# A fused attention and feed-forward kernel: the row's threshold word moves from VectorE to GpSimd

## The chip, the cores and the metric

One core of one Trainium2 chip runs the whole program. The metric is device time in microseconds of one execution. The profile names the engines PE (TensorE, its weight loads as PEld), DVE (VectorE), ACT (ScalarE), POOL (GpSimd) and SP (SyncE, which here only issues transfers).

## What is computed

Attention in which a row keeps only the scores within `tau` of its maximum, over 8 batches of 8 heads, 576 positions, 64 dimensions, and behind it a dense layer pair of 512 to 2048 to 512 with the activation h * tanh(softplus(h)), in float32:

```
scores = scale * q @ k^T                       # per head 576 x 576
thresh = max(scores, axis=-1) - tau
scores = where(scores >= thresh, scores, -1e9)
attn   = exp(scores - max(scores)); attn = attn / (sum(attn) + 1e-9)
x      = (attn @ v), heads side by side        # 4608 tokens x 512
h      = x @ w_in                              # 512 -> 2048
out    = (h * tanh(log1p(exp(h)))) @ w_out     # 2048 -> 512
```

## The kernel before

Attention works on pairs of heads. A pair is cut into 9 tiles of 128 query rows, 32 pairs give 288 tiles (`NT`), and the loop over `g` in `attention_moe` issues one tile's stages per turn, each stage some turns behind the one before. Between them it hands out the first matrix product of earlier batches (`gemm1`, through `advance`), so that TensorE has work while a tile passes through the other engines. After the last tile come the rest of `gemm1` and the second product, which have no attention work beside them.

Every engine runs its instructions in the order in which the loop issues them: `Engines` wraps TensorE, VectorE, ScalarE and GpSimd, and `InOrder` ties each instruction to the one before it on its engine. Its `method(...)` call is line 95, so nearly every row of the profile reads L95 and is told apart by its tiles.

What tile `g` goes through, by the names in the profile:

- `scores` writes the 128 x 576 scores to one of two PSUM buffers `s`. TensorE can start tile g+2 only when tile g's buffer has been read by the masking.
- `row_max` (VectorE, `st<-s`, TENSOR_REDUCE) puts the negated row maximum into word 0 of `st`, a small tile of 8 words a row, of which three exist in turn.
- `exponential` makes two words from it: the exponential's bias (word 2, `st<-st`) and the threshold (word 1, `st<-st,back`, where `back` holds tau in unscaled units). Then ScalarE writes `e<-s,st`.
- `masked` (VectorE, `p<-s,st,e`, SCALAR_TENSOR_TENSOR) compares the scores with the threshold, multiplies by `e` and sums the row. From tile 54 (`UNV`) on GpSimd then makes a 128x1 word `un` of the sum (`st<-st` on POOL), before that VectorE makes it in `total`.
- `normalise` (VectorE RECIPROCAL, then GpSimd `p<-p,st`, 128x576) scales the tile; it is issued one turn later, so in turn g it scales tile g-1.
- `transposes`, two turns behind, turns `p` into `tp` and `t`; ScalarE and VectorE split these into `hi`, `lo` and `tk` three turns behind; `values` multiplies by v into `y`, and the results are gathered by `x<-x,yo` on GpSimd.

GpSimd also makes the low parts of the loaded q, k and v (`q<-r,q`, `k<-r,k`, `vs<-r,vs`), of x (`xl<-x,xh`) and, up to about 200 us, of the first weights (`w1l<-dec,w1h`, `dec<-dec`).

In one turn of the loop the calls that matter stand in this order, after `begin(g + 1)` for early tiles: row_max(g), total(g-1), exponential(g), normalise(g-1), the split parts of tile g-3, the gathers and low parts, masked(g), and then `gemm1` with `begin(g + 1)` in its middle.

Of the kernel before, what the change touches and what calls it, by code (L numbers as in the profile page):

```python
# [9 lines left out]
ALU = mybir.AluOpType  # L10
# [175 lines left out]
def attention_moe(tc, q, k, v, tau, w_in, w_out, out):  # L186
    nc = tc.nc
    from contextlib import ExitStack

    with ExitStack() as outer:  # L190
# [8 lines left out]
        back = cst.tile([P, 1], F32, name="back")  # L199

        nc = Engines(tc)
        with ExitStack() as first:
# [21 lines left out]
            with ExitStack() as att:  # L224
# [22 lines left out]
                def rows(x, step):  # L247

                    flat = x.rearrange("p a b -> p (a b)")
                    return flat[:, :2 * step].rearrange("p (a b) -> p a b", a=2)[:, :, :HL]  # L250
# [162 lines left out]
                def exponential(s, st, e):  # L413
                    nm = st[:, 0:1]
                    nc.vector.tensor_scalar(st[:, 2:3], nm, SCALE, None, ALU.mult)
                    nc.vector.tensor_scalar(st[:, 1:2], nm, -1.0, back, ALU.mult, ALU.subtract)
                    nc.scalar.activation(rows(e, HL), rows(s, 512 - 2 * G), AF.Exp, bias=st[:, 2:3], scale=SCALE)

                def masked(g, s, st, e, p):
# [224 lines left out]
                for g in range(NT + 5):  # L644
# [32 lines left out]
                    if g < NT:  # L677
                        exponential(tiles[g]["s"], tiles[g]["st"], tiles[g]["e"])
# [384 lines left out]
```

## Time and profile before

| | |
|---|---|
| Runs | 1316.25, 1318.91, 1318.0 us, median 1318.0 us |
| Profiled execution | 1316.2 us, of it 1314.4 us span |
| TensorE clock granted | 0.998 of full speed |
| Busy share of the span | PE 98%, PEld 94%, DVE 87%, ACT 78%, POOL 57% |
| Threshold word on VectorE | 288 instructions, 204 ns each |
| 128x1 word `un` on GpSimd | 234 instructions, 220 ns each |
| Scaling on GpSimd | 288 instructions, 836 ns each |

The span runs from the first to the last instruction. Attention fills it to about 900 us; the rest is the second product. A row in order of time gives start and duration in microseconds, the engine, the operation, what it writes from what it reads, a count, and in brackets the idle time ahead of it with what ended that. A group gives its busy time and the mean in ns, then the idle time ahead of all its members and what ended most of it. A wait gives the sum, how often, and the longest.

### The profile page before, as it was taken

Reading aid. Unit: us, or ns where it says so; the run is one execution under the profiler, and the core shown is the slowest. Engines: PE = TensorE matmul, PEld = TensorE weight load, DVE = VectorE, ACT = ScalarE, POOL = GpSimd, SP = SyncE. Lnnn points to the kernel's source line nnn. Section 1 sums busy time; section 2 is a strip of 40 time slices with the busy share of each in tenths; the row PEclk is TensorE's granted clock in tenths of the full one; section 3 lists DMA queues with packets and bytes.
Section 4 is the critical chain, followed back from the end, with each engine's and each line's share of the span. In section 5 each row is a group of like instructions: output and inputs, shape, how many; then the busy total and the mean of one; then the engine's idle time right before and its main releaser. Section 6 shows DMA issues by size and latency. Waiting matters only on the chain.

```text
span 1314.4 us, 30410 instructions
## 1 busy us (share of the span) xinstructions
PE 1282.1 (98%) x9875; PEld 1241.6 (94%) x9875; DVE 1140.2 (87%) x2943; ACT 1029.1 (78%) x2320; POOL 746.0 (57%) x1080
## 2 busy tenths in 40 slices
PE   8998899999999999999999999999999999999998
PEld 7766899999999999999999999999999999999998
DVE  7999999999999999999999999997978666778764
ACT  6889888888888888888888888877767667567562
POOL 4779888888788887888888888774100000000000
PEclk9999999999999999999999999999999999999999
DMA  5334455444444444444445444425645454553440
GB/s 187 114 104 139 150 152 147 129 126 143 127 148 134 139 130 131 148 138 132 136 125 155 129 138 143 118 91 168 226 141 158 124 139 135 161 153 111 115 121 33
DMA packets 171917, 178.68 MB, mean 136 GB/s; under 512 B 46576, under 2 KB 139760, under 8 KB 171504
## 3 DMA queue, kind: packets, MB, share of 16 engines
q1 hardware_dynamic: 171760, 176.74, 45.4%
q8 instruction: 79, 1.29, 0.4%
q14 instruction: 78, 0.64, 0.2%
HBM read 109.05 MB, written 49.28 MB: 120 GB/s over the span
## 4 chain that ended last, share of the span: by engine, by line
PE 70%; DVE 17%; ACT 9%; issue 4%; POOL 0%; DMA 0%; SPq 0%; DVEq 0%; ACTq 0%; POOLq 0%
PE h L95 20%; PE y L95 15%; PE x L95 11%; PE s L95 8%; PE z L95 7%; DVE st L95 6%; PE tp L95 6%; DVE p L95 4%; ACT e L95 3%; DVE dec L95 2%; DVE lo L95 2%; PE hx L95 1%; ACT hi L95 1%; DVE tk L95 1%; ACT dec L95 1%
## 5 line engine op out<-in xcount | busy, mean ns | idle before, releaser
L95 PE MATMUL h<-xh,w1h 128*128 128x288 f32 x976 | 295.0, 302 | 2.5 <-ACT yo L95 1.1
L95 PE MATMUL h<-xh,w1l 128*128 128x288 f32 x976 | 292.4, 300 | 0.0
L95 PE MATMUL h<-xl,w1h 128*128 128x288 f32 x976 | 288.3, 295 | 0.3 <-DVE xl L95 0.3
L95 POOL TENSOR_SCALAR p<-p,st 128x576 f32<-128x576 f32 x288 | 240.9, 836 | 65.0 <-DVE st L95 42.1
L95 ACT ACTIVATE e<-s,st 128x580 f32<-128x580 f32 x288 | 215.0, 747 | 62.3 <-DVE st L95 56.6
L95 DVE SCALAR_TENSOR_TENSOR p<-s,st,e 128x580 f32<-128x580 f32 x288 | 236.2, 820 | 18.9 <-ACT e L95 7.3
L95 DVE TENSOR_REDUCE st<-s 128x1 f32<-128x580 f32 x288 | 217.8, 756 | 0.9
L95 PE MATMUL s<-k,q 128*128 128x290 f32 (+1 forms) x1056 | 196.2, 309 | 9.5 <-DVE p L95 8.8
L95 DVE TENSOR_TENSOR ring<-un,ring 128x512 fp32r<-128x512 f32 x252 | 156.8, 683 | 53.6 <-ACT ring L95 53.6
L95 DVE TENSOR_TENSOR lo<-tp,hi 128x512 fp32r<-128x512 f32 (+1 forms) x280 | 173.1, 627 | 25.1 <-ACT hi L95 22.9
L95 PEld LDWEIGHTS h<-xh,w1h 128*128 128x128 f32 x976 | 184.0, 188 | 6.4 <-ACT yo L95 4.2
L95 PEld LDWEIGHTS h<-xl,w1h 128*128 128x128 f32 x976 | 183.8, 188 | 0.5 <-DVE xl L95 0.5
L95 PEld LDWEIGHTS h<-xh,w1l 128*128 128x128 f32 x976 | 183.7, 188 | 0.0
L95 PE MATMUL tp<-ident,p 128*128 128x128 f32 x1152 | 173.8, 273 | 10.1 <-DVE lo L95 5.6
L95 PEld LDWEIGHTS s<-k,q 128*128 128x128 f32 x1056 | 157.6, 189 | 22.8 <-DVE p L95 19.7
L95 ACT CAST hi<-tp 128x512 fp32r<-128x512 f32 (+1 forms) x280 | 150.0, 546 | 35.5 <-PE tp L95 31.6
L95 ACT CAST ring<-un 128x512 fp32r<-128x512 f32 x252 | 138.3, 618 | 33.7 <-DVE un L95 32.8
L95 PEld LDWEIGHTS tp<-ident,p 128*128 128x128 f32 x1152 | 137.7, 140 | 21.8 <-POOL k L95 6.9
L95 PE MATMUL x<-ring,un 128*128 128x256 f32 x1296 | 154.6, 278 | 0.6 <-ACT ring L95 0.6
L95 PEld LDWEIGHTS x<-ring,un 128*128 128x128 f32 x1296 | 152.1, 188 | 0.8 <-ACT ring L95 0.8
L95 PE MATMUL y<-hi,vs 128*128 128x256 f32 (+1 forms) x448 | 132.0, 317 | 3.0 <-ACT hst L95 2.4
L95 PE MATMUL y<-lo,vs 128*128 128x256 f32 (+1 forms) x448 | 121.8, 295 | 0.0
(88 smaller groups left out, 2570.9 us busy)
## 6 DMA issues: line engine op xcount, KB each, us to landing
hd<-hst SPq DMA_DIRECT2D x128, 288.0 KB, 2.6
r<-q SPq DMA_DIRECT2D x120, 160.0 KB, 2.6
r<-k SPq DMA_DIRECT2D x120, 160.0 KB, 2.2
out_t<-ost SPq DMA_DIRECT2D x36, 256.0 KB, 2.2
r<-v SPq DMA_DIRECT2D x56, 160.0 KB, 2.3
dec<-w_in SPq DMA_DIRECT2D x32, 256.0 KB, 2.8
un<-hd SPq DMA_DIRECT2D x16, 512.0 KB, 5.4
kph<-k SPq DMA_DIRECT2D x56, 144.0 KB, 3.0
```

The source lines that it names most:

```text
L95: made = method(*args, **kwargs)
```

## The change

The threshold word is issued on GpSimd instead of VectorE, at the same place in the code. The operation and its operands stay.

```
@@ exponential(s, st, e)
                     nm = st[:, 0:1]
                     nc.vector.tensor_scalar(st[:, 2:3], nm, SCALE, None, ALU.mult)
-                    nc.vector.tensor_scalar(st[:, 1:2], nm, -1.0, back, ALU.mult, ALU.subtract)
+                    nc.gpsimd.tensor_scalar(st[:, 1:2], nm, -1.0, back, ALU.mult, ALU.subtract)
                     nc.scalar.activation(rows(e, HL), rows(s, 512 - 2 * G), AF.Exp, bias=st[:, 2:3], scale=SCALE)
```

Since `exponential(g)` is called ahead of `normalise(g-1)`, the word stands on GpSimd behind the word `un` of tile g-1 and ahead of the scaling of tile g-1. The masking of tile g, which stayed on VectorE, reads it from there. The order on TensorE, ScalarE and SyncE is the same as before.

On GpSimd, in the middle of attention (the stretch about 399 to 408 us of the profile before), first before:

```order
L95 TENSOR_TENSOR x<-x,yo 64x320
L95 TENSOR_TENSOR q_6198<-r,q_6198 64x320 x2
L95 TENSOR_SCALAR st<-st 128x1
L95 TENSOR_SCALAR p<-p,st 128x576
L95 TENSOR_SCALAR st<-st 128x1
L95 TENSOR_SCALAR p<-p,st 128x576
L95 TENSOR_TENSOR x<-x,yo 64x320
L95 TENSOR_TENSOR q_6201<-r,q_6201 64x320
L95 TENSOR_SCALAR st<-st 128x1
L95 TENSOR_SCALAR p<-p,st 128x576
```

and now, on the same engine and at the same place:

```order
L95 TENSOR_TENSOR x<-x,yo 64x320
L95 TENSOR_TENSOR q_6198<-r,q_6198 64x320 x2
L95 TENSOR_SCALAR st<-st 128x1
L95 TENSOR_SCALAR st<-st,back 128x1
L95 TENSOR_SCALAR p<-p,st 128x576
L95 TENSOR_SCALAR st<-st 128x1
L95 TENSOR_SCALAR st<-st,back 128x1
L95 TENSOR_SCALAR p<-p,st 128x576
L95 TENSOR_TENSOR x<-x,yo 64x320
L95 TENSOR_TENSOR q_6201<-r,q_6201 64x320
L95 TENSOR_SCALAR st<-st 128x1
L95 TENSOR_SCALAR st<-st,back 128x1
```

A 128x1 instruction has come between the word `un` and the scaling in each tile; the splits and gathers ahead of them in the queue are those of before.

On VectorE over the same tiles, before (`lo`, `tk` are the split parts of an older tile):

```order
L95 TENSOR_REDUCE st<-s_141 128x1
L95 TENSOR_SCALAR st<-st 128x1
L95 TENSOR_SCALAR st<-st,back 128x1
L95 RECIPROCAL st<-st 128x1
L95 TENSOR_TENSOR lo<-tp,hi 128x4x128
L95 SCALAR_TENSOR_TENSOR p,st<-s_141,st,e_142 128x580
L95 TENSOR_REDUCE st<-s_135 128x1
L95 TENSOR_SCALAR st<-st 128x1
L95 TENSOR_SCALAR st<-st,back 128x1
```

and now, on VectorE over these tiles:

```order
L95 TENSOR_REDUCE st<-s_141 128x1
L95 TENSOR_SCALAR st<-st 128x1
L95 RECIPROCAL st<-st 128x1
L95 TENSOR_TENSOR lo<-tp,hi 128x4x128
L95 SCALAR_TENSOR_TENSOR p,st<-s_141,st,e_142 128x580
L95 TENSOR_REDUCE st<-s_135 128x1
L95 TENSOR_SCALAR st<-st 128x1
L95 RECIPROCAL st<-st 128x1
```

The reciprocal, on which the scaling on GpSimd waits, now stands one instruction earlier; the masking (`p,st<-...`) waits for a word from another engine.

More of the change, by code (lines that the diff above doesn't have):

```diff
@@ L415, in exponential @@
                     nc.vector.tensor_scalar(st[:, 2:3], nm, SCALE, None, ALU.mult)
-                    nc.vector.tensor_scalar(st[:, 1:2], nm, -1.0, back, ALU.mult, ALU.subtract)
+                    nc.gpsimd.tensor_scalar(st[:, 1:2], nm, -1.0, back, ALU.mult, ALU.subtract)
                     nc.scalar.activation(rows(e, HL), rows(s, 512 - 2 * G), AF.Exp, bias=st[:, 2:3], scale=SCALE)
```

## The prediction

> **What bounds the kernel now.** I read the page's head first, then the table of busy time by stretch, then the waits of the long attention stretch, then the order of time on VectorE, GpSimd and TensorE over three tiles.
>
> ```profile
> span 1314.4 us, 30410 instructions
> PE 1282.1 (98%) x9875; PEld 1241.6 (94%) x9875; DVE 1140.2 (87%) x2943; ACT 1029.1 (78%) x2320; POOL 746.0 (57%) x1080
> ...
> core 0: us, PE busy (x) PEld busy (x) DVE busy (x) ACT busy (x) POOL busy (x), PEclk, DMA share, GB/s
> 0.00:100.00 100.00, 91.62 (x504) 72.15 (x504) 86.14 (x306) 77.39 (x193) 66.37 (x87) 1.00 0.44 135
> 100.00:200.00 100.00, 88.58 (x598) 79.81 (x598) 95.19 (x297) 85.37 (x221) 89.00 (x114) 0.98 0.50 146
> 200.00:870.00 670.00, 663.72 (x5095) 652.66 (x5094) 627.08 (x1837) 579.46 (x1408) 562.38 (x839) 1.00 0.46 136
> 870.00:1314.00 444.00, 438.23 (x3684) 436.98 (x3682) 331.76 (x507) 286.83 (x501) 28.24 (x42) 1.00 0.46 134
> ```
>
> The mean of 57% for GpSimd hides two stages. From 870 us on it does almost nothing, and of the 288 tiles only 9 are left there (288 less the 61 and 218 counted below), which I leave out. From 200 to 870 us TensorE is 99% busy and sets the pace, VectorE is at 94% and GpSimd at 84%. From 100 to 200 us TensorE is at 89%, VectorE at 95%, GpSimd at 89%: there the two helpers set the pace. So the question is how much room GpSimd really has.
>
> ```profile
> L95 POOL TENSOR_SCALAR p<-p,st 128x576 f32<-128x576 f32 x218 | 180.4, 828 | 38.3 <-DVE st L95 19.9 <-DMA kph<-k 1.7 <-PE y L95 0.4
> L95 POOL TENSOR_SCALAR st<-st 128x1 f32<-128x1 f32 x218 | 48.0, 220 | 19.9 <-DVE p L95 0.5
> ...
> POOL x L95 <- ACT yo L95: 35.2, 46, 1.2
> ACT e L95 <- DVE st L95: 29.1, 53, 1.4
> POOL p L95 <- DVE st L95: 19.9, 37, 0.9
> PEld s L95 <- DVE p L95: 0.4, 1, 0.4
> ```
>
> These are GpSimd's groups and the waits from 200 to 870 us: 218 tiles, so 3.07 us a tile. Of the 107.6 us in which GpSimd isn't busy (670 - 562.4), 19.9 us stand ahead of the 128x1 instruction with almost no releaser: 0.09 us of issue each. The waits with a name come to 35.2 + 19.9 + 1.7 and a few small ones, which I put at 62 us, 0.28 us a tile. That is all the room there is. TensorE waits for a masked tile once in this stretch (0.4 us).
>
> **The change part by part.** Three tiles in order of time, the three engines mixed:
>
> ```profile
> 399.88 1.72 POOL L95 TENSOR_TENSOR q<-r,q 64x320 fp32r<-64x320 f32 x2
> 401.51 0.82 DVE L95 SCALAR_TENSOR_TENSOR p<-s,st,e 128x580 f32<-128x580 f32 x1
> 401.69 0.22 POOL L95 TENSOR_SCALAR st<-st 128x1 f32<-128x1 f32 x1
> 402.00 0.82 POOL L95 TENSOR_SCALAR p<-p,st 128x576 f32<-128x576 f32 x1
> 402.26 0.76 DVE L95 TENSOR_REDUCE st<-s 128x1 f32<-128x580 f32 x1
> 402.91 0.21 POOL L95 TENSOR_SCALAR st<-st 128x1 f32<-128x1 f32 x1
> 403.05 0.15 DVE L95 TENSOR_SCALAR st<-st 128x1 f32<-128x1 f32 x1
> 403.12 0.20 DVE L95 TENSOR_SCALAR st<-st,back 128x1 f32<-128x1 f32 x1
> 403.24 0.15 DVE L95 RECIPROCAL st<-st 128x1 f32<-128x1 f32 x1
> 403.43 0.69 DVE L95 TENSOR_TENSOR lo<-tp,hi 128x512 fp32r<-128x512 f32 x1
> 403.57 0.82 POOL L95 TENSOR_SCALAR p<-p,st 128x576 f32<-128x576 f32 x1 [0.45 <-DVE st L95]
> 404.44 0.69 PE L95 MATMUL s<-k,q 128*128 128x290 f32 x4
> 404.78 0.82 DVE L95 SCALAR_TENSOR_TENSOR p<-s,st,e 128x580 f32<-128x580 f32 x1
> 405.63 0.87 POOL L95 TENSOR_TENSOR x<-x,yo 64x320 f32<-64x320 f32 x1 [1.24 <-ACT yo L95]
> 406.32 0.29 PE L95 MATMUL s<-kph,qph 128*128 128x290 f32 x1
> 406.46 0.88 POOL L95 TENSOR_TENSOR q<-r,q 64x320 fp32r<-64x320 f32 x1
> 407.34 0.82 DVE L95 SCALAR_TENSOR_TENSOR p<-s,st,e 128x580 f32<-128x580 f32 x1
> 407.43 0.21 POOL L95 TENSOR_SCALAR st<-st 128x1 f32<-128x1 f32 x1
> ```
>
> What VectorE gains: the threshold word starts at 403.12 and the reciprocal at 403.24, so its place in the queue is worth 0.12 us and not its 0.20 us. Over 288 tiles that is 35 us of VectorE's time. From 200 us on it lies beside TensorE, which is the bound, so I cost it at nothing there; its cover is TensorE's 99%.
>
> What GpSimd pays: the nearest row is its own 128x1 instruction, 0.22 us long. The scaling behind it starts 0.31 us after it does (401.69 to 402.00), so I take 0.31 us a tile: 218 x 0.31 = 67.6 us from 200 to 870 us. The lower end is its duration alone, 218 x 0.22 = 48 us; the upper end is the row of the early stage below, 0.43 us, 94 us. The threshold word has a tensor as second operand, which the nearest row has not; on VectorE that made 0.20 out of 0.15 us, so the lower end is unlikely. The Trainium skill, Perfetto Trace Analysis, section GPSIMD Engine Instruction, says that a GpSimd instruction's reported span is unreliable and should be timed by start-to-start spacing. By spans alone GpSimd would need 48 us of its 62 us of waits and the main stage would cost nothing; by spacing it needs more than it has. The rows agree with spacing.
>
> The new wait: VectorE's masking step now waits for GpSimd, and behind it in VectorE's queue stand the next row maximum, the exponential's bias and the split parts. At 401.51 us the masking ran while GpSimd was still at the two q splits (399.88 + 1.72 = 401.60). With the change the word could run only behind the 128x1 at 401.69, about where the scaling stands at 402.00, and end at 402.2: the masking starts 0.7 us late. For the next tile the word is ready about 403.5, a microsecond ahead of the masking at 404.78. For the one at 407.34 GpSimd is busy to 407.34 and its 128x1 starts at 407.43, so the word ends near 408.0, again 0.65 us late. Such delays don't reach TensorE at once: the masking that ends at 402.33 (401.51 + 0.82) frees the bank of the scores that start at 404.44, 2.1 us of slack, and the one that ends at 405.60 the scores at 406.32, 0.7 us. So a late tile is absorbed as long as GpSimd catches up. That it doesn't, on average, is what costs.
>
> How much of the 62 us GpSimd can use: the waits for yo (35.2 us in 46, 0.77 us each) come once in 4.7 tiles, in which the new instruction adds 1.46 us, so they vanish whole. The waits for the reciprocal (19.9 us in 37) hang on the same row maximum that the new word waits for, and if the masking is late that moves too; I let a third vanish, 7 us. With 4 us of the small ones, 46 us are used: 67.6 - 46 = 21.6 us longer. The bounds are 5.6 us (all 62 used) and 67.6 us (none).
>
> The early stage, up to 200 us, where most tiles have no other 128x1 on GpSimd:
>
> ```profile
> 148.68 1.72 POOL L95 TENSOR_TENSOR q<-r,q 64x320 fp32r<-64x320 f32 x2
> 150.47 0.74 POOL L95 TENSOR_TENSOR w1l<-dec,w1h 128x256 fp32r<-128x256 f32 x1
> 151.19 0.98 POOL L95 TENSOR_SCALAR p<-p,st 128x576 f32<-128x576 f32 x1
> ...
> L95 POOL TENSOR_SCALAR p<-p,st 128x576 f32<-128x576 f32 x29 | 25.1, 864 | 2.8 <-DVE st L95 2.2
> ...
> L95 POOL TENSOR_SCALAR p<-p,st 128x576 f32<-128x576 f32 x61 | 53.1, 870 | 22.3 <-DVE st L95 19.9 <-DVE dec L95 1.5
> ...
> PEld s L95 <- DVE p L95: 19.9, 30, 1.7
> PE s L95 <- DVE p L95: 9.0, 16, 1.5
> ```
>
> The first three rows are GpSimd back to back: the scaling starts 0.02 us before the step ahead of it ends. With an issue gap of 0.09 us on both sides the word would push it by about 0.42 us. From 100 to 200 us there are 29 tiles (the first count): 12 us more work against 11 us that GpSimd isn't busy. The second count and the waits below it are of the stretch from 0 to 200 us: TensorE waits 28.9 us there for masked tiles, so here time on the helpers is time of the kernel. The first 32 tiles (61 - 29) leave GpSimd room (66% busy), and half of VectorE's 32 x 0.12 us may show: -2 us. For the second hundred I let half the 12 us show: +6 us. Together +4 us, between -7 us (61 x 0.12, all gained) and +12 us.
>
> Sum: 1316.2 us (1314.4 us of span and 1.8 us around it) + 21.6 + 4 = 1341.8 us. The median of the runs shown, 1318.0 us, lies 1.8 us above the profiled execution: 1343.6, say 1344 us, 2.0% slower.
>
> **The rivals.**
> Absorbed: the word costs GpSimd no more than its waits, 0.22 us or less, and the 0.7 to 2.1 us of slack ahead of the scores take what is left. Then 1318 us, within about 3 us; it speaks for it that TensorE waited 0.4 us for masked tiles from 200 to 870 us. 0.2% is about what a measurement can tell from no change.
> Faster: VectorE's relief shows wherever TensorE waited for it. The place is the first 200 us, the price 61 x 0.12 = 7 us: 1311 us. It decides for this if GpSimd comes to the word before VectorE gets to the masking, as in the tile at 404.78; two tiles out of three above speak against.
> Lockstep: GpSimd has to wait for each row maximum and VectorE for GpSimd in each tile, so no wait is used up: +68 +10 us, 1396 us. The uneven work between two scalings speaks for it (two splits ahead of 401.69, none ahead of 402.91), the slack of 0.7 to 2.1 us against.
> Blocked port: GpSimd's word and VectorE's bias word start on the same row maximum, and one could hold the other up by 0.15 to 0.22 us. Over 61 early tiles that is at most 13 us, 1357 us with the forecast. The 128x1 at 402.91 on GpSimd ran beside the one at 403.05 on VectorE, and neither was longer than usual:
>
> ```profile
> L95 DVE TENSOR_SCALAR st<-st x217: 153/154/157, 203.5 to 867.4; 128x1 f32<-128x1 f32 x109
> ```
>
> The Trainium skill, SBUF — State Buffer, section Who interferes with whom, says that a VectorE instruction in a two-port mode and a GpSimd instruction lock each other out for the whole of it. The longest of 217 here is 157 ns, so no row bears the lock out for these shapes.
>
> **How the numbers follow.** Chances: the forecast (1327 to 1375 us, from a main stage between +5.6 and about +50) 0.64; lockstep (1375 to 1400) 0.12; blocked port on top 0.04; absorbed 0.10; faster 0.10. Absorbed splits into 0.08 within 0.2% and 0.02 slower. Slower 0.64 + 0.12 + 0.04 + 0.02 = 0.82. The range leaves out the faster case and the far part of lockstep: 1318 to 1380 us; the forecast's own is 1327 to 1375.
>
> **What would show it.** Right: from 200 us on the same work takes about 22 us longer, GpSimd is over 90% busy there, its waits for yo nearly gone, and a new wait of VectorE's p for GpSimd's st leads the list. TensorE's share in that stage falls to about 96%, with waits of s for p. The stage from 870 us on keeps its length. Wrong: if the new 128x1 group has no gap of its own around it, if VectorE's p waits little for it, or if the scalings start earlier, the sum falls to the rival it points to.

## The result and the profile after

The changed kernel takes 1379.98 us (median; 1379.79 to 1380.73) against 1317.99 us: a ratio of 1.0474, 95% interval 1.0459 to 1.0490, 62.0 us slower. The prediction had 26 us. Page head, chain and the table of busy time by stretch of the kernel after, with the stretches set so that the middle one holds about as many tiles:

```profile
span 1378.9 us, 30197 instructions
PE 1310.5 (95%) x9875; PEld 1248.2 (91%) x9875; DVE 1105.1 (80%) x2655; ACT 1023.1 (74%) x2320; POOL 833.7 (60%) x1368
...
PE 34%; DVE 32%; POOL 15%; ACT 11%; issue 6%; DMA 1%; POOLq 0%; SPq 0%; DVEq 0%; ACTq 0%
...
0.00:100.00 100.00, 90.23 (x491) 70.84 (x491) 81.33 (x263) 75.02 (x186) 72.74 (x116) 1.00 0.43 130
100.00:200.00 100.00, 87.45 (x547) 77.64 (x546) 87.13 (x254) 79.91 (x204) 89.86 (x131) 0.93 0.47 137
200.00:920.00 720.00, 681.06 (x5059) 649.83 (x5057) 593.99 (x1608) 570.24 (x1404) 626.06 (x1050) 1.00 0.42 126
```

The chain that ended last ran on TensorE for 34% of the span; before, this line read:

```profile
PE 70%; DVE 17%; ACT 9%; issue 4%; POOL 0%; DMA 0%; SPq 0%; DVEq 0%; ACTq 0%; POOLq 0%
```

From 200 us on no engine is busy all the time: TensorE fell from 99% to 95%, VectorE from 94% to 82%, and GpSimd rose only from 84% to 87%. Of GpSimd's 93.9 us that aren't busy, waits with a name make up about 44 us; the rest are short gaps without one. The engines wait for each other. Groups of GpSimd and waits from 200 to 920 us:

```profile
L95 POOL TENSOR_SCALAR p<-p,st 128x576 f32<-128x576 f32 x216 | 179.6, 832 | 1.3 <-POOL st L95 0.3
L95 POOL TENSOR_SCALAR st<-st,back 128x1 f32<-128x1 f32 x216 | 66.3, 307 | 29.5 <-DVE st L95 11.7
L95 POOL TENSOR_SCALAR st<-st 128x1 f32<-128x1 f32 x217 | 50.9, 235 | 21.3 <-DVE p L95 0.8
...
ACT e L95 <- DVE st L95: 117.3, 156, 2.3
DVE p L95 <- POOL st L95: 80.0, 91, 2.6
POOL x L95 <- ACT yo L95: 26.0, 46, 0.9
PEld s L95 <- DVE p L95: 14.7, 18, 1.5
```

216 tiles in 720 us are 3.33 us a tile; before, 218 in 670 us were 3.07. The difference, 0.26 us, times 218 is 57 us. Counted by the start of the 62nd masking (197.8 us before, 207.6 now) and of the 280th (868.5 and 933.8), the change costs 9.8 us up to the first and 55.5 us between the two; behind them nothing is added. (The two profiled spans lie 64.5 us apart, a little more than the medians.) The new wait of VectorE's masking for GpSimd leads VectorE's own waits with 80.0 us, and the exponential's wait for VectorE went from 29.1 to 117.3 us. GpSimd still waits 26.0 us for yo (35.2 before). Two turns of the loop in order of time, GpSimd, VectorE and ScalarE mixed, some rows left out:

```profile
449.18 0.87 POOL L95 TENSOR_TENSOR vs<-r,vs 128x320 fp32r<-128x320 f32 x1
450.15 0.24 POOL L95 TENSOR_SCALAR st<-st 128x1 f32<-128x1 f32 x1
450.48 0.30 POOL L95 TENSOR_SCALAR st<-st,back 128x1 f32<-128x1 f32 x1
450.76 0.83 POOL L95 TENSOR_SCALAR p<-p,st 128x576 f32<-128x576 f32 x1
450.82 0.82 DVE L95 SCALAR_TENSOR_TENSOR p<-s,st,e 128x580 f32<-128x580 f32 x1 [0.95 <-POOL st L95]
451.56 1.15 DVE L95 SCALAR_TENSOR_TENSOR dec<-dec 128x256 uint32<-128x256 uint32 x1
452.64 0.75 DVE L95 TENSOR_REDUCE st<-s 128x1 f32<-128x580 f32 x1
453.43 0.15 DVE L95 TENSOR_SCALAR st<-st 128x1 f32<-128x1 f32 x1
453.68 0.74 ACT L95 ACTIVATE e<-s,st 128x580 f32<-128x580 f32 x1 [2.24 <-DVE st L95]
454.75 0.42 ACT L95 COPY yo<-y 64x320 f32<-64x320 f32 x1
455.25 0.87 POOL L95 TENSOR_TENSOR x<-x,yo 64x320 f32<-64x320 f32 x1 [0.42 <-ACT yo L95]
```

This is a ring. GpSimd comes late to the threshold word (450.48), so VectorE stands idle for 0.95 us ahead of the masking; behind the masking in VectorE's queue stand the next row maximum and bias word (453.43), so ScalarE stands idle for 2.24 us ahead of the exponential; behind that in ScalarE's queue stands the copy yo (454.75); and for yo GpSimd, late itself, waits another 0.42 us. In this turn a step of the second weights (`dec`, 1.15 us) also stands between the masking and the row maximum; only 16 of the 216 tiles have one. Without it the links are the same: at 511.59 us a masking started after 0.96 us of idle time, the exponential at 513.38 after 1.86 us, and the gather at 514.96 after 0.22 us of waiting for yo.

### The profile page after: what moved, and what is told of

Read it like the earlier page. It is cut to its first block, busy times and chain, and to the rows that moved or that the text cites. A ratio compares the mean times of both kernels' runs of the same rounds, so it can differ in the third digit from the quotient of the medians.

```text
span 1378.9 us, 30197 instructions
## 1 busy us (share of the span) xinstructions
PE 1310.5 (95%) x9875; PEld 1248.2 (91%) x9875; DVE 1105.1 (80%) x2655; ACT 1023.1 (74%) x2320; POOL 833.7 (60%) x1368
## 4 chain that ended last, share of the span: by engine, by line
PE 34%; DVE 32%; POOL 15%; ACT 11%; issue 6%; DMA 1%; POOLq 0%; SPq 0%; DVEq 0%; ACTq 0%
DVE st L95 13%; DVE p L95 12%; PE x L95 11%; PE y L95 8%; PE z L95 7%; PE h L95 5%; ACT e L95 5%; POOL st L95 4%; POOL q L95 4%; DVE lo L95 3%; POOL k L95 2%; DVE tk L95 2%; DVE dec L95 2%; POOL p L95 1%; PE hx L95 1%
## 5 line engine op out<-in xcount | busy, mean ns | idle before, releaser
L95 PE MATMUL s<-k,q 128*128 128x290 f32 (+1 forms) x1056 | 200.4, 314 | 20.4 <-DVE p L95 20.1
```

What stands on the lines that cost most here:

```text
L95: made = method(*args, **kwargs)
```

## The experiments

Three theories were set against each other. Load: 0.31 us a tile is more work than GpSimd has room for, whoever reads the word. Wait: the masking's new wait closes the ring, whatever GpSimd's work. Both: each is small alone. Each ratio is against runs of the kernel before that were measured beside it (medians 1317.46 to 1318.56 us). The cuts of code show the lines that matter of each edit.

**Added work alone** (on the kernel before; 4:5 is a spare word).

```
                     nc.vector.tensor_scalar(st[:, 1:2], nm, -1.0, back, ALU.mult, ALU.subtract)
+                    nc.gpsimd.tensor_scalar(st[:, 4:5], nm, -1.0, back, ALU.mult, ALU.subtract)
```

> VectorE still computes the threshold word and the masking still reads that one; GpSimd computes the same word at the place of the changed kernel, into a spare word that nobody reads. So GpSimd has the whole added work and nobody waits for it. Load theory (GpSimd is full, and 0.31 us a tile is simply too much work): 1365 to 1385 us, as the changed kernel or slower, since VectorE keeps its word too. Wait theory (the masking's new wait closes a ring from VectorE over GpSimd and ScalarE back to VectorE, so that no wait on GpSimd can be used up): 1318 to 1328 us. Both needed: between 1328 and 1350 us.

Measured: 1333.78 against 1318.04 us, ratio 1.0123 (1.0108 to 1.0138), 15.7 us. Waits from 200 to 880 us:

```profile
ACT xh L95 <- POOL x L95: 21.9, 12, 2.3
...
POOL x L95 <- ACT yo L95: 1.9, 4, 0.5
```

GpSimd's wait for yo is gone, 1.9 for 35.2 us: the new work has used up nearly all of GpSimd's room. GpSimd is late now (ScalarE waits 21.9 us for its x), but no one waits for the word. The load theory's 1365 us is ruled out; the time lies in the range set for "both needed".

**Relief of VectorE alone** (on the kernel before; `...` stands for lines left out).

```
-                    nc.vector.tensor_scalar(st[:, 1:2], nm, -1.0, back, ALU.mult, ALU.subtract)
...
-                    th, su, un = (st[:, i:i + 1] for i in (1, 3, 5))
+                    th, su, un = back, *(st[:, i:i + 1] for i in (3, 5))
```

> The threshold word is computed by nobody; the masking compares with the constant tau word instead, so the output is another. It prices VectorE's relief alone. If TensorE is the bound from 200 us on, only the first 200 us gain: 1311 to 1316 us. If VectorE's queue paces the main stage too, more: down to 1290 us.

Measured: 1314.29 us, ratio 0.9976 (0.9967 to 0.9986). The 35 us of VectorE's time are worth 3.8 us. That is what this relief is worth by itself.

**The wait alone** (on the kernel before).

```
                     th, su, un = (st[:, i:i + 1] for i in (1, 3, 5))
+                    if g > UNV:
+                        th = tiles[g - 1]["st"][:, 5:6]
```

> GpSimd does no more than before, VectorE still computes the threshold word; but from tile 55 on the masking takes as its threshold the 128x1 word that GpSimd makes anyway for the tile before (so the output is another). That gives the masking a wait for GpSimd's queue at nearly the place of the changed kernel, with no added work. Load theory: 1316 to 1321 us. Wait theory: at least half of the loss, 1345 us or more. Both needed: 1321 to 1340 us.

Measured: 1341.67 us, ratio 1.0184 (1.0169 to 1.0199), 23.6 us, just between the ranges of "both needed" and of the wait theory. With not one instruction more on GpSimd, the wait costs more than the work. Waits from 200 to 880 us:

```profile
ACT e L95 <- DVE st L95: 67.6, 96, 1.8
...
POOL x L95 <- ACT yo L95: 33.1, 57, 1.0
DVE p L95 <- POOL st L95: 24.2, 40, 1.5
```

The ring stands here too: the masking waits 24.2 us for GpSimd, the exponential 67.6 us, and GpSimd's wait for yo stays at 33.1 us. Work alone and wait alone add up to 39.3 us; the change costs 62.0, so 22.7 us come only with both (26.5, if the relief of 3.8 us is set against them, which neither of the two runs has). A part of that lies in the early tiles, since this run has no wait before tile 55: up to the 62nd masking the change costs 9.8 us, the work alone 5.1, the wait alone 1.3. Between the 62nd and the 280th they cost 55.5, 13.1 and 24.3 us, so 18 us come only with both there.

**The two words exchanged** (on the changed kernel).

```
-UNV = 54
+UNV = 300
```

> The changed kernel, with the word of the row sum that GpSimd makes from tile 54 on given back to VectorE for all tiles. So from tile 54 on GpSimd and VectorE do as many 128x1 words as before, but the masking waits for GpSimd. Load theory: only the first 54 tiles lose, about 8 us: 1322 to 1328 us. Wait theory: 1350 us or more. Both needed: 1328 to 1345 us.

Measured: 1343.20 us, ratio 1.0194 (1.0178 to 1.0209). It came out where "both needed" was set, at its upper edge: 25 us remain. Not all of them are the wait's, since the first 54 tiles still carry the added word. Up to the 62nd masking 8.1 us are lost, which is what the load theory gave for the early tiles; between the 62nd and the 280th, where GpSimd's count of words is that of before, 18.5 us are lost (24.3 with the wait alone).

**The word ahead of the other one** (on the changed kernel).

```
-                def normalise(st, p):
+                def normalise(g, st, p):
                     su, un, rc = (st[:, i:i + 1] for i in (3, 5, 6))
+                    if g >= UNV:
+                        nc.gpsimd.tensor_scalar(un, su, FLOOR, 1.0 / S, ALU.is_le, ALU.mult)
```

(the same two lines are taken out of `masked`)

> The changed kernel, but on GpSimd the word of the row sum (tile g-1) is issued behind the threshold word of tile g instead of ahead of it. The work of every engine is that of the changed kernel; the threshold word is ready 0.33 us earlier in each tile in which GpSimd is late. Load theory: no change, 1378 to 1382 us. Ring theory (the masking waits for GpSimd, the next row maximum and exponential for the masking, ScalarE's copies behind the exponential, and GpSimd's gather for those): the 91 waits of the masking from 200 to 920 us get shorter by up to 0.33 us each, 1350 to 1370 us.

Measured: 1376.93 us, ratio 1.0448 (1.0432 to 1.0463), 3 us less than the changed kernel: a miss for the ring theory's number. From 200 to 920 us a group and a wait of GpSimd, and then the masking's group, first of the changed kernel and then of this one:

```profile
L95 POOL TENSOR_SCALAR p<-p,st 128x576 f32<-128x576 f32 x217 | 179.2, 826 | 22.8
...
POOL x L95 <- ACT yo L95: 8.6, 26, 0.6
...
L95 DVE SCALAR_TENSOR_TENSOR p<-s,st,e 128x580 f32<-128x580 f32 x216 | 177.5, 822 | 103.3 <-POOL st L95 80.0 <-ACT e L95 10.7 <-ACT hi L95 7.6
L95 DVE SCALAR_TENSOR_TENSOR p<-s,st,e 128x580 f32<-128x580 f32 x218 | 179.2, 822 | 104.4 <-POOL st L95 66.2 <-ACT tk L95 18.3 <-ACT e L95 7.4
```

GpSimd waits less for yo (8.6 for 26.0 us), but the scaling now stands right behind the word that it needs, and the idle time ahead of it rose from 1.3 to 22.8 us: 17 us won, 21 us given back in gaps without a name. The masking's idle time didn't fall: 104.4 for 103.3 us, though less of it is put down to GpSimd. So an earlier place in a queue that stays as long won next to nothing.

**The gather on VectorE** (on the changed kernel).

```
-                            adds.append(values(LAST[t], pr["pt"], pr["ops"]["vs"], pr["x"], nc.vector if g >= NT - 1 else nc.gpsimd))
+                            adds.append(values(LAST[t], pr["pt"], pr["ops"]["vs"], pr["x"], nc.vector))
```

> The changed kernel with the gather x<-x,yo on VectorE instead of GpSimd. It takes 97 instructions, 77 us, and the wait for ScalarE from GpSimd's queue, and gives VectorE about 97 x 0.4 = 39 us. Ring theory and load theory both: most of the loss gone, 1318 to 1335 us, and the masking's wait for GpSimd under 20 us. If VectorE's queue becomes the bound instead, 1335 to 1355 us.

Measured: 1414.96 us, ratio 1.0734 (1.0717 to 1.0752). A miss for the number of both theories and for the third range. The masking's wait for GpSimd did fall as forecast, to 8.4 us; but the wait that GpSimd lost stands in VectorE's queue now, ahead of the masking, and is longer there (200 to 920 us):

```profile
ACT e L95 <- DVE st L95: 141.3, 175, 2.0
DVE x L95 <- ACT yo L95: 67.6, 89, 1.8
```

GpSimd is busy for only 75% of this stretch (87% in the changed kernel), so its amount of work doesn't set this time. The gather itself took 0.50 us on VectorE, 46 us in all.

**The word read one turn late** (on the changed kernel).

```
                     th, su, un = (st[:, i:i + 1] for i in (1, 3, 5))
+                    if g:
+                        th = tiles[g - 1]["st"][:, 1:2]
```

> The changed kernel, but the masking of tile g compares with the threshold word of tile g-1, so that the word is wanted a turn later (the output is another). Work and order on all engines are those of the changed kernel; only the wait has one turn more of slack. Ring theory: the loss falls to that of the added work alone, 1326 to 1336 us (1334 us was measured with the word on both engines). Load theory: stays at 1375 us or more.

Measured: 1333.99 us, ratio 1.0124 (1.0109 to 1.0139). Work, order and engines are those of the changed kernel, and 46 of the 62 us are gone. The two waits from 200 to 880 us, a stretch that holds 217 tiles here, as 200 to 920 us held 216 in the changed kernel:

```profile
DVE p L95 <- POOL st L95: 6.0, 10, 0.8
...
POOL x L95 <- ACT yo L95: 2.1, 4, 0.6
```

Both waits fall together, 80.0 to 6.0 and 26.0 to 2.1 us. GpSimd's waits with a name, about 44 us in the changed kernel, are down to 5. What is left is about the 16 us of work alone (that run lacked VectorE's relief, so up to 4 us may still be the wait's). This is the run that settles it: with the same work in the same order, the added work is absorbed only while nobody waits for it in the same turn.

**The word on ScalarE** (on the changed kernel; `back` is negated).

```
-                    nc.gpsimd.tensor_scalar(st[:, 1:2], nm, -1.0, back, ALU.mult, ALU.subtract)
+                    nc.scalar.activation(st[:, 1:2], nm, AF.Identity, bias=back, scale=-1.0)
```

> The threshold word is made by ScalarE, just ahead of the exponential, which the masking waits for anyway: VectorE's relief with no new wait on a third queue, and 288 x about 0.2 us more on ScalarE, of it what the exponential comes later. Ring theory: 1313 to 1322 us, near the kernel before. If the exponential's delay reaches the masking in each tile: up to 1340 us.

Measured: 1324.63 us, ratio 1.0050 (1.0035 to 1.0065), above the ring theory's range and well under the second one's 1340. The word takes 295 ns on ScalarE, not 0.2 us. A word on a queue that the masking waits for anyway costs 6.7 us, a tenth of what the change costs.

**A second spare word** (on the kernel with added work alone).

```
+                    nc.gpsimd.tensor_scalar(st[:, 7:8], nm, -1.0, back, ALU.mult, ALU.subtract)
```

> The kernel with the word on both engines and nobody waiting for GpSimd's, with a second such spare word on GpSimd. The first one cost 16 us, since GpSimd's 62 us of waits took in most of it. If that room is used up, as the waits left there say (about 5 us), the second costs nearly its whole 0.31 us a tile: 1390 to 1425 us. If GpSimd still has room, 1345 to 1370 us.

Measured: 1394.20 us, ratio 1.0578 (1.0561 to 1.0596): 60 us for the second word after 16 for the first. From 200 to 940 us GpSimd has no wait with a name left. The room on GpSimd was about one word wide.

**Two ways to do without the word's own instruction.** The first masks by `e` against exp(-tau), the second makes both words in one 128x2 instruction on VectorE (`sign` holds -1 and the scale, `back` tau and 0). Of the first the cut shows the masking alone; its threshold word goes, and `back` is turned into exp(-tau) once.

```
-                    nc.vector.scalar_tensor_tensor(to, s[:, :, :HL], th, rows(e, HL + 2 * G), ALU.is_ge, ALU.mult, accum_out=su)
+                    e = rows(e, HL + 2 * G)
+                    nc.vector.scalar_tensor_tensor(to, e, back, e, ALU.is_ge, ALU.mult, accum_out=su)
```

> No threshold word on any engine: the masking keeps an element where its exponential e is at least exp(-tau), a constant of the run, which it reads with e instead of the scores. VectorE has one 128x1 less per tile, GpSimd no more than before, and the score buffer is free after the exponential. Ring theory and load theory: no new wait and no new work, so at or under the relief alone (1314 us was measured): 1308 to 1316 us, the early waits of the scores for the masking gone. If reading e twice from one memory makes the masking itself longer than 0.82 us, or holds GpSimd up, slower than before: 1320 to 1345 us.

```
-                    nc.vector.tensor_scalar(st[:, 2:3], nm, SCALE, None, ALU.mult)
-                    nc.vector.tensor_scalar(st[:, 1:2], nm, -1.0, back, ALU.mult, ALU.subtract)
+                    nc.vector.scalar_tensor_tensor(st[:, 1:3], sign, nm, back, ALU.mult, ALU.subtract)
```

> The kernel before, with VectorE making both 128x1 words of the row maximum, threshold and bias, in one 128x2 instruction (a constant pair times the maximum less a second pair). No work moves to another engine and no wait is added; VectorE loses 0.12 us a tile as in the kernel without the word, which took 1314 us. Both theories expect 1312 to 1316 us, a gain of 0.2 to 0.4%. If the 128x2 form is longer than the two together, or the bias comes later for the exponential: 1318 to 1325 us.

Measured: 1373.36 us, ratio 1.0431 (1.0415 to 1.0446), and 1361.91 us, ratio 1.0331 (1.0317 to 1.0345). Neither beats the kernel before. Both give VectorE an instruction with two inputs in SBUF in every tile, which the last section shows to be held up beside GpSimd, so neither tests the theories. What they would win without that isn't shown; the relief alone is worth 3.8 us.

**The gather one turn later**, on the changed kernel and, as its base, on the kernel before.

```
-                    while adds:
-                        adds.pop(0)()
+                    while sums:
+                        sums.pop(0)()
+                    while adds:
+                        sums.append(adds.pop(0)())
```

(`gather` returns its last step instead of issuing it; after the last tile both are issued at once)

> The changed kernel, but GpSimd's gather x<-x,yo is issued one turn of the loop later, when ScalarE's copy yo should long be there. The work of all engines stays. Ring theory: the 26 us that GpSimd waits for yo from 200 to 920 us fall under 5 us, and the time falls with them: 1345 to 1362 us. If the loss is set by GpSimd's work and the masking's wait alone, whatever GpSimd waits for: 1375 to 1382 us.

> The kernel before with the same later gather, as the base for the run with the changed kernel. GpSimd isn't waited for here, so both theories expect no change, 1315 to 1320 us.

Measured: 1405.92 us, ratio 1.0669 (1.0651 to 1.0686), and the base 1360.20 us, ratio 1.0324 (1.0305 to 1.0343). Both missed. ScalarE's copies of x, in order in its queue, now wait for the later gather (200 to 900 us of the base):

```profile
ACT xh L95 <- POOL x L95: 37.2, 23, 2.4
```

On this base the change costs 45.7 us instead of 62.0. GpSimd has no wait for yo left in either kernel, and yet the masking waits 66.3 us for GpSimd in the first (200 to 920 us). So most of the loss stays without the yo leg of the ring. The base is so different (1360.20 us, a clock of 0.987 granted in its profile and 0.982 with the change) that the run doesn't price that leg by itself.

## Why the prediction was wrong

Its sign, its place and its wait were right; its size was too small by 36 us (62.0 measured, 25.6 summed). Nearly all of that lies in the long stage, summed at 21.6 us and measured at 55.5 between the 62nd and the 280th masking. The tiles ahead of it were summed at 4 us and cost 9.8, inside the bounds given.

The step that failed is "The waits for yo ... so they vanish whole", and with it the 46 us of GpSimd's 62 us of waits that the sum let the new work use. The waits for yo went from 35.2 to 26.0 us only. All of GpSimd's waits with a name after the change, 26.0 + 11.7 and small ones, are about 44 us: 18 us were used, not 46. That is 28 of the 34 us that the long stage's sum lacked. The argument was sound for work that nobody waits for: with the added work alone, and with the word read one turn late, 5 us of these waits are left (1333.8 and 1334.0 us). It took the moment at which ScalarE delivers yo as fixed, when the masking's delay moves ScalarE too. For the other class of waits, those for the row maximum, the same text did see this, "if the masking is late that moves too"; it failed to ask it of yo.

"A late tile is absorbed as long as GpSimd catches up" was the second error, in the reading of slack. The 0.7 to 2.1 us ahead of TensorE's scores were real, but a late masking does not only reach TensorE through the scores; it reaches the next row maximum and the exponential at once. The wait alone, with no more work on GpSimd, cost 24 us where this sentence gives about nothing.

The price of the word was nearly right: 0.31 us by spacing, and the words at 450.15 and 450.48 with the scaling at 450.76 put 0.61 us where 0.31 stood. Over the whole stage GpSimd's busy time and its gaps without a name rose from 2.79 to 3.13 us a tile, 74 us for the 67.6 of the sum; that is most of what is left of the 34. (The upper end of 0.43 us isn't a row, but about the 0.42 us estimated for the early stage.) VectorE's relief was right in being small: 3.8 us alone, where the faster rival had 7; in its one trace the gain doesn't lie in the first 200 us, where that rival put it. The lockstep rival, "no wait is used up", with 0.12, was nearer to the mechanism than the forecast; at 1396 us it was too high, since 18 us were used, and VectorE waited for GpSimd in 91 of 216 tiles, not in each. The time fell into its span of 1375 to 1400 us; that it is still inside the range given, 1318 to 1380 us, by 0.02 us is luck, since the forecast's own part ended at 1375. Of a blocked port, the last section finds 4.6 us.

Of the signs named in advance, the masking's new wait came (second to the exponential's in the list), TensorE at 96% came (95%, with waits of s for p, 14.7 us of them at the weight loads), and the last stage kept its length. "Its waits for yo nearly gone" and GpSimd "over 90% busy" did not come (26.0 us, 87%). Those two showed the failed step.

What stays open is by which path the 22.7 us arise that come only with work and wait together. The yo wait differs by 24 us between the changed kernel and the work alone, and reading the word a turn later removes both; that fits the ring. But the word ahead of the other one took 17 us of the yo wait away for 3 us of time, and the later gather took all of it away, on another base, with 45.7 us of loss left. So the same-turn wait is shown to be the cause, and the part of the yo leg in it is not.

## What to carry to other kernels

Before an engine's idle time is counted as room, follow each of its waits back: a wait whose source will move with the delay that you add is not room. A small word made on a loaded queue costs little if it is read a turn later and much if it is read in the same turn; the added work (16 us), the wait (24 us) and the two together (62 us) are three prices, and the wait can be priced without the work by making the reader depend on something that the queue already produces. Moving a waiting instruction to another queue moves the wait ahead of what stands there: with the gather on VectorE the time rose from 1380 to 1415 us.

## What the runs showed of the hardware

A VectorE instruction with two tensors from SBUF and GpSimd's instructions held each other up. With the masking by `e` alone, groups from 200 to 900 us:

```profile
L95 DVE SCALAR_TENSOR_TENSOR p<-e,back 128x580 f32<-128x580 f32 x213 | 213.5, 1002 | 19.4 <-ACT e L95 15.7
...
L95 POOL TENSOR_SCALAR p<-p,st 128x576 f32<-128x576 f32 x212 | 196.4, 927 | 19.7 <-DMA kph<-k 0.2
...
L95 POOL TENSOR_SCALAR st<-st 128x1 f32<-128x1 f32 x212 | 80.8, 381 | 19.0
```

The masking takes 1002 ns, 821 when it reads the scores from PSUM; GpSimd's scaling 927 for 828 and its word 381 for 220 ns. With both words in one instruction, in order of time and over 200 to 900 us (shortest, median, longest):

```profile
432.75 0.88 POOL L95 TENSOR_TENSOR k<-r,k 128x320 fp32r<-128x320 f32 x1
433.08 0.57 DVE L95 SCALAR_TENSOR_TENSOR st<-sign,st,back 128x2 f32<-128x2 f32 x1
...
L95 DVE SCALAR_TENSOR_TENSOR st<-sign,st,back x217: 220/298/1574, 201.0 to 898.4; 128x2 f32<-128x2 f32 x109
```

Two elements a row take from 220 to 1574 ns; the one at 433.08 ends with GpSimd's split, 433.65 and 433.63 us. The exponential waits for it. By the same trace, the 41 of these words that start with no GpSimd instruction running take 220 to 243 ns, and the 108 that take over 300 ns all end within 0.06 us of the end of a GpSimd instruction. The masking by `e` takes as little as 814 ns, so it isn't slower by its form. The Trainium skill, SBUF — State Buffer, section Who interferes with whom, says that a VectorE instruction with two SBUF inputs contends with a GpSimd instruction that reads SBUF, and that the order of issue decides which of them blocks. These rows agree; the longest word, from 494.94 to 496.51 us, stood behind two GpSimd instructions in a row, of which the second ended at 496.49. The word that the change moves is no such instruction, and VectorE's words of one input stayed at 153 to 157 ns in the kernel after (216 of them from 200 to 920 us). Both kernels hold a few: 16 steps `dec<-dec` with two inputs in the long stage, 608 ns each before and 895 after, 4.6 us more in all.
